# Attention on one core: the output stores go from SyncE's queue to GpSimd's, a pair of heads at a time

## The chip, the core and the metric

The kernel runs on one core of a Trainium2 chip. The core has TensorE (matrix products), VectorE, ScalarE (activations) and GpSimd for computing, and SyncE, which here only issues DMAs. SyncE, ScalarE and GpSimd can each issue DMAs; 16 DMA engines carry them out. Every engine works through its own instructions in order, and waits on semaphores for the others. The metric is the device time of one execution in microseconds (us); less is better. Before the change it is 1190.38 us, the median of three runs (1185.31, 1190.38 and 1191.48).

## The reference

```
B, H, Sq, Sk, D = 16, 32, 192, 1024, 128          # q, k, v in bfloat16
scores = einsum("bhqd,bhkd->bhqk", q, k) * D**-0.5
p      = softmax(scores, axis=-1)
return   einsum("bhqk,bhkd->bhqd", p, v)
```

There are 16 x 32 = 512 heads. Each has 192 queries, 1024 keys and 1024 values of 128 numbers. The inputs are 25.2 MB of q, 134.2 MB of k and 134.2 MB of v; the output is 25.2 MB.

## The kernel before

**Tiling.** 512 heads are 32 groups (`NGR`) of 16 heads (`G`), and a group is 8 pairs of heads (`PPG`). A pair has 2 x 192 = 384 queries, which are three units of 128: A (the first 128 of head a), B (the last 128 of head b) and S (64 left over from each). Two pairs make six units, A0 B0 A1 B1 S0 S1, and one *period* of the order that is written out by hand in `PE_ORDER`, `DVE_ORDER` and `ACT_ORDER` (lines 17 to 20). A tick behind a name there means that the step belongs to the period before, two ticks the one before that. So a group is four periods and 24 units (`UPG`).

**A unit's way.** TensorE makes its scores into `s_ps` (`qk`). VectorE copies them to `ss`, scaled and negated, and takes the row maximum (`rowmax`, L333). For units A0 and B1 GpSimd subtracts the maximum (`shift`, L208) and ScalarE takes the exponential later; for the other four ScalarE does both at once (`exp_first`, L374). TensorE transposes the result into `pt_ps` (`tr`), ScalarE brings it to `pt_sb` (`evac`, L383 and L385), and TensorE multiplies it with the values into `o_ps` (`pv`). When the three units of a pair are done, VectorE divides by the row sums and writes the pair's output to `ob` (`outputs`, L358), which adds one to the semaphore `s_on`.

**Buffers.** The transposed keys `kt` and queries `qt`, the values `vs` and the outputs `ob` have two buffers each, for two groups.

**DMA queues.** SyncE issues the loads of K (L148) and Q (L152), both as DMA transposes, and the stores (L172). Its program is: the first loads; then for each group g, `loads(g + 2)`, which waits until TensorE has made the last scores of group g (`s_qk`), and `stores(g, 0, 8)`, which waits until all outputs of group g are in `ob`. So behind the loads of a group stand the stores of the group two before it, and the next loads stand behind these. A group's output is 128 partitions of 8 x 3 rows of 256 bytes. It is stored as three DMAs, over partitions 0 to 79, 80 to 123 and 124 to 127 (`STORE_PARTS`). The last group is stored in four steps over all partitions as its pairs come out.

ScalarE issues the loads of V from group 2 on (L138, called at L394): in the middle of group g - 1, behind the evacuation of its thirteenth unit, it waits for the last PV product of group g - 2 (L392) and for K of group g to have landed (L393), and then issues V of group g. While it waits there, nothing else runs on ScalarE.

VectorE waits, before the first output of a group (L354), for the stores of the group that had the same half of `ob`. GpSimd does nothing but two shifts a period.

Of the kernel before, what the change touches and what calls it, by code (L numbers as in the profile page):

```python
# [22 lines left out]
def _order(text, periods):  # L23
    ops = [(w.split(":")[0], w.split(":")[1].rstrip("'"), w.count("'")) for w in text.split()]
    for p in range(periods + max(back for _, _, back in ops)):
        for op, name, back in ops:
            if 0 <= p - back < periods:
                if name in UNITS:
                    yield op, 6 * (p - back) + UNITS.index(name)
                else:  # L30
                    yield op, 2 * (p - back) + int(name)


def _attention_kernel(nc, q, k, v, out, G=16, NS=2, NSS=5, NX=4, NPT=5,
                      FIRST=((0, 2), (2, 8), (8, 16)), LAST=((0, 4), (4, 6), (6, 7), (7, 8)), STORE_PARTS=((0, 80), (80, 124), (124, 128)), VALUES_AFTER=("ev", 12)):
    B, H, SQ, D = q.shape
    SK = k.shape[2]
    assert D == 128 and SK == 1024 and SQ == 192, (D, SK, SQ)
# [2 lines left out]
    NGR = NH // G  # L41
    PPG = G // 2
# [5 lines left out]
    NSO = 2  # L48
# [5 lines left out]
    of = out.rearrange("b h s d -> (b h) s d")  # L54

    def shifted(u):
        return UNITS[u % 6] in SHIFTED
# [12 lines left out]
    with ExitStack() as es:  # L70
        def sb(name, shape, dt):
            return es.enter_context(nc.sbuf_tensor(name, shape, dt))
# [4 lines left out]
        def sem(name):  # L77
            return es.enter_context(nc.semaphore(name))
# [4 lines left out]
        ob = sb("ob", [128, NSO, PPG, 3, 128], BF16)  # L83
# [14 lines left out]
        svl = [sem("svl%d" % i) for i in range(NS)]  # L98
        sf = [sem("sf%d" % i) for i in range(len(FIRST))]
        sfv = [sem("sfv%d" % i) for i in range(len(FIRST))]  # L100
        sst = [sem("sst%d" % i) for i in range(NSO)]
        s_qk = sem("s_qk")
        s_max = sem("s_max")
        s_xa = sem("s_xa")
# [5 lines left out]
        s_on = sem("s_on")  # L110
# [3 lines left out]
        def unit_info(u):  # L114
            name = UNITS[u % 6]
            pr = 2 * (u // 6) + int(name[1])
            return pr, "ABS".index(name[0]), pr // PPG, pr % PPG
# [7 lines left out]
            return 16 * (g // NS + 1 - (g % NS == 0))  # L125

        def store_cnt(g):
            return 16 * len(STORE_PARTS) * (g // NSO + 1)

        def wait_x(eng, u):  # L130
            eng.wait_ge(s_xp if shifted(u) else s_xa, x_cnt[u])

        def pair_units(pr):
            return [u for u in range(6 * (pr // 2), 6 * (pr // 2) + 6) if unit_info(u)[0] == pr]

        def load_v(e, g, a, b, sm):
            h0 = g * G
            e.dma_start(  # L138
                vs[:, g % NS, a:b],
                vf[h0 + a:h0 + b].rearrange("g (p t) d -> p g t d", t=KT_TILES),  # L140
            ).then_inc(sm, 16)

        @block.sync
        def _(e):
            def load_kq(g, a, b, sems):
                s = g % NS
                h0 = g * G
                e.dma_start_transpose(  # L148
                    kt[:, s, :, a * 128:b * 128],
                    kf[h0 + a:h0 + b].rearrange("g (p t) d -> (g p) (t d)", t=KT_TILES),  # L150
                ).then_inc(sems[0], 16)
                e.dma_start_transpose(  # L152
                    qt[:, s, a * SQ:b * SQ],
                    qf[h0 + a:h0 + b].rearrange("g r d -> (g r) d"),
                ).then_inc(sems[1], 16)

            def loads(g):
                s = g % NS
                last_u = (g - NS + 1) * UPG - 1
                if g >= NS:  # L160
                    e.wait_ge(s_qk, last_u + 1)
                load_kq(g, 0, G, (sxk[s], sxq[s]))
                if g < NS:
                    load_v(e, g, 0, G, svl[s])

            def stores(g, a, b):
                so = g % NSO
                e.wait_ge(s_on, g * PPG + b)
                rows = of[g * G + 2 * a:g * G + 2 * b].rearrange("h r d -> (h r) d").rearrange(
                    "(n p) d -> p n d", p=128)  # L170
                for lo, hi in (((0, 128),) if g == NGR - 1 else STORE_PARTS):
                    e.dma_start(  # L172
                        rows[lo:hi],
                        ob[lo:hi, so, a:b].rearrange("p pg y d -> p (pg y) d"),
                    ).then_inc(sst[so], 16)

            n = len(FIRST)
            for i in range(n):
                load_kq(0, *FIRST[i], (sf[i], sf[i]))
                if i > 0:  # L180
                    for i2 in range(i if i > 1 else 0, i + 1):
                        load_v(e, 0, *FIRST[i2], sfv[i2])
            for g in range(1, min(NS, NGR)):
                loads(g)
            for g in range(NGR):
                if g + NS < NGR:
                    loads(g + NS)
                for a, b in (LAST if g == NGR - 1 else ((0, PPG),)):
                    stores(g, a, b)
            for so in range(min(NSO, NGR)):  # L190
                n = len(range(so, NGR - 1, NSO)) * len(STORE_PARTS)
                if so == (NGR - 1) % NSO:
                    n += len(LAST)
                e.wait_ge(sst[so], 16 * n)

        @block.gpsimd
        def _(gp):
            gp.memset(ones[:], 1.0).then_inc(s_setup, 1)  # L198
            gp.wait_ge(s_setup, 1)
            gp.affine_select(  # L200
                ident[:], ones[:], [[1, 128]], ALU.is_equal, 0.0, base=0, channel_multiplier=-1
            ).then_inc(s_setup, 1)

            def shift(u):
                gp.wait_ge(s_max, u + 1)
                if u >= NX:
                    gp.wait_ge(s_tr, u - NX + 1)
                gp.tensor_tensor(  # L208
                    x_sb[:, u % NX, :], ss[:, u % NSS, :],
                    nb[:, u % NSS: u % NSS + 1].to_broadcast([128, SK]), ALU.subtract,  # L210
                ).then_inc(s_xp, 1)

            for u in range(NU):
                if shifted(u):
                    shift(u)

        @block.tensor
        def _(pe):
# [19 lines left out]
            def qk(u):  # L238
# [13 lines left out]
                if g == 0:  # L252
                    for i, (h, _) in enumerate(FIRST):
                        if h <= b and i not in seen_kq:
# [72 lines left out]
        @block.vector  # L327
        def _(dve):
            def rowmax(u):
                dve.wait_ge(s_qk, u + 1)  # L330
                if u >= NSS and UNITS[u % 6] == "S1":
                    wait_x(dve, u - NSS)
                dve.tensor_scalar(  # L333
                    ss[:, u % NSS, :], s_ps[u % 2][:].rearrange("p t k -> p (t k)"), -scale, None, ALU.mult, ALU.min,
                    accum_out=nb[:, u % NSS: u % NSS + 1],
                ).then_inc(s_max, 1)

            def slots_of(pr, way):
                slots = sorted(O_SLOT[unit_info(u)[1]] for u in pair_units(pr) if shifted(u) == way)
                return slice(slots[0], slots[-1] + 1)  # L340

            def sums(pr):

                dve.wait_ge(s_xa, max(x_cnt[u] for u in pair_units(pr) if not shifted(u)))
                sel = slots_of(pr, False)
                dve.reciprocal(rinv[:, pr % 2, sel], rs[:, pr % NRS, sel]).then_inc(s_ri, 1)  # L346

            def outputs(pr):
                g = pr // PPG
                pg = pr % PPG  # L350
                so = g % NSO
                dve.wait_ge(s_pv, max(pv_cnt[u] for u in pair_units(pr)))
                if pg == 0 and g >= NSO:
                    dve.wait_ge(sst[so], store_cnt(g - NSO))  # L354
                sel = slots_of(pr, True)
                dve.reciprocal(rinv[:, pr % 2, sel], o_ps[pr % 2][:, 3, sel]).then_inc(s_ri, 1)  # L356
                dve.wait_ge(s_ri, 2 * pr + 2)
                dve.tensor_tensor(  # L358
                    ob[:, so, pg],
                    o_ps[pr % 2][:, 0:3, :],  # L360
                    rinv[:, pr % 2, 0:3].unsqueeze(2).to_broadcast([128, 3, 128]),
                    ALU.mult,
                ).then_inc(s_on, 1)

            do = {"max": rowmax, "sum": sums, "out": outputs}
            for op, u in _order(DVE_ORDER, NU // 6):
                do[op](u)
# [65 lines left out]
```

## Time and profile before

| | |
|---|---|
| median of three runs | 1190.38 us |
| the profiled execution, time | 1188.88 us |
| the profiled execution, span | 1187.1 us |
| granted clock of TensorE | 0.993 |
| TensorE products / VectorE / ScalarE / GpSimd busy | 1125.9 / 1087.6 / 1080.6 / 485.8 us |
| DMA traffic | 321.26 MB, mean 271 GB/s |
| queue q1 (SyncE): K, Q, stores, first V loads | 728257 packets, 192.95 MB |
| queue q10 (ScalarE): V loads | 61920 packets, 125.83 MB |

The page also lists who waited for whom. TensorE's busy time is modelled from pipelined products, so its 95% does not say that it is at its peak. A DMA issue shown on SyncE's queue lasts until SyncE can go on to its next instruction, not until the data has landed. The DMA share in a stretch of time adds up packets and can pass 1. The stores' landing times are not told by the page.

### The profile page before, as it was taken

The numbers are of one execution on the slowest core, as the hardware profiler recorded it, in microseconds if no ns is written. First come the engines' busy times: TensorE is split into PE (matmuls) and PEld (weight loads), VectorE is DVE, ScalarE is ACT, GpSimd is POOL, SyncE is SP. The second block draws the span as 40 slices with busy tenths as digits, with TensorE's granted clock in tenths as the row PEclk, the third lists the DMA queues.
The fourth block names the chain that finished last, engine by engine and source line by source line (L and its number), as shares of the span: only waits on it lengthen the run. The fifth ranks groups of instructions, "written<-read, shape, count | busy, mean of one in ns | idle before, by whom it ended". The sixth has DMA issues, their size and how long they took to land.

```text
span 1187.1 us, 38884 instructions
## 1 busy us (share of the span) xinstructions
PE 1125.9 (95%) x18432; PEld 845.9 (71%) x15360; DVE 1087.6 (92%) x2304; ACT 1080.6 (91%) x1793; POOL 485.8 (41%) x262
## 2 busy tenths in 40 slices
PE   5699999999999999999999999999999999999998
PEld 2477776777777776777777767777777776677776
DVE  5589998999999998999999989999999999899997
ACT  4679998999999998999999988999999998899998
POOL 2234443444444434443444434344444343444442
PEclk9899999999999999999999999999999999999999
DMA  9999999999999999999999999999999999999981
GB/s 231 249 280 303 289 285 254 260 299 293 287 293 248 256 290 288 280 283 258 279 298 284 284 265 242 290 296 282 288 266 267 295 284 290 259 267 277 297 246 40
DMA packets 790348, 321.26 MB, mean 271 GB/s; under 512 B 724641, under 2 KB 724641, under 8 KB 790177
## 3 DMA queue, kind: packets, MB, share of 16 engines
q1 hardware_dynamic: 728257, 192.95, 84.0%
q10 hardware_dynamic: 61920, 125.83, 28.7%
q8 instruction: 132, 2.16, 0.7%
q14 instruction: 39, 0.32, 0.1%
HBM read 134.22 MB, written 25.17 MB: 134 GB/s over the span
## 4 chain that ended last, share of the span: by engine, by line
PE 43%; DMA 39%; ACT 11%; SPq 5%; ACTq 1%; issue 0%; DVE 0%
DMA kt<-in_k_dram 39%; PE o_ps L221 15%; PE pt_ps L221 15%; PE s_ps L221 14%; ACT x_sb L374 6%; SPq L148 4%; ACT pt_sb L385 3%; ACT pt_sb L383 2%; ACTq L138 1%; SPq L152 1%; SPq L138 0%; DMA vs<-in_v_dram 0%; DVE ob L358 0%; ACTq L393 0%; DVE rinv L356 0%
## 5 line engine op out<-in xcount | busy, mean ns | idle before, releaser
L333 DVE TENSOR_SCALAR_CACHE_REDUCE ss<-s_ps 128x1024 f32<-128x1024 f32 x768 | 919.5, 1220 | 83.2 <-PE s_ps L221 69.7
L208 POOL TENSOR_TENSOR x_sb<-ss,nb 128x1024 bf16<-128x1024 f32 x256 | 485.1, 1895 | 689.3 <-DVE ss L333 574.1
L374 ACT ACTIVATE x_sb<-ss,nb 128x1024 bf16<-128x1024 f32 x512 | 584.9, 1144 | 13.0 <-DVE ss L333 13.0
L306 PEld LDWEIGHTS <-pt_sb 128*128 128x128 bf16 (+1 forms) x8192 | 440.9, 104 | 194.9 <-issue 101.7
L221 PE MATMUL o_ps<-vs,pt_sb 128*128 128x128 bf16 (+1 forms) x8192 | 494.9, 219 | 0.4 <-DMA vs<-in_v_dram 0.3
L221 PE MATMUL s_ps<-kt,qt 128*128 128x512 bf16 (+1 forms) x2048 | 465.2, 385 | 24.2 <-DMA qt<-in_q_dram 23.7
L221 PE MATMUL pt_ps<-ident,x_sb 128*128 128x128 bf16 x6144 | 449.9, 220 | 33.4 <-ACT pt_sb L383 15.9
L280 PEld LDWEIGHTS <-x_sb 128*128 128x128 bf16 x6144 | 368.9, 98 | 101.5 <-issue 100.7
L385 ACT ACTIVATE pt_sb<-pt_ps 128x512 f32<-128x512 f32 x512 | 306.3, 598 | 84.6 <-PE pt_ps L221 51.5
L383 ACT ACTIVATE pt_sb<-pt_ps 128x1024 bf16<-128x1024 bf16 x256 | 260.3, 1017 | 3.6 <-PE pt_ps L221 3.6
L221 PE MATMUL o_ps<-ones,pt_sb 128*128 128x1 bf16 x2048 | 189.3, 165 | 0.0
L358 DVE TENSOR_TENSOR ob<-o_ps,rinv 128x384 bf16<-128x384 f32 x256 | 142.6, 557 | 8.7
L264 PEld LDWEIGHTS <-qt 128*128 128x128 bf16 (+1 forms) x1024 | 79.3, 103 | 41.6 <-DMA qt<-in_q_dram 18.7
L374 ACT ACTIVATION_READ_ACCUMULATOR x_sb<-ss,nb 128x1 f32 x512 | 100.3, 196 | 0.0
L333 DVE DVE_READ_ACCUMULATOR ss<-s_ps 128x1 f32 x768 | 63.7, 83 | 0.0
L356 DVE RECIPROCAL rinv<-o_ps 128x1 f32<-128x1 f32 x256 | 41.8, 163 | 4.3 <-PE o_ps L221 4.3
L346 DVE RECIPROCAL rinv<-rs 128x2 f32<-128x2 f32 x256 | 41.0, 160 | 1.1 <-ACT x_sb L374 1.1
L374 ACT ACT_TABLE_LOAD x1 | 1.3, 1283 | 0.8 <-PEq L418 0.8
L200 POOL TENSOR_SCALAR_AFFINE_SELECT ident<-ones 128x128 bf16<-128x128 bf16 x1 | 0.3, 294 | 0.1
L198 POOL MEMSET ones<- 128x128 bf16 x1 | 0.2, 205 | 0.3 <-POOLq L418 0.3
L418 POOL MEMSET const-float32-0.0<- 128x1 f32 x1 | 0.1, 99 | 0.3 <-issue 0.3
L418 POOL MEMSET const-bfloat16-1.0<- 128x1 bf16 x1 | 0.1, 102 | 0.0
(2 smaller groups left out, 0.2 us busy)
## 6 DMA issues: line engine op xcount, KB each, us to landing
vs<-in_v_dram ACTq DMA_DIRECT2D x30, 4096.0 KB, 16.3
out_dram<-ob SPq DMA_DIRECT2D x31, 480.0 KB
out_dram<-ob SPq DMA_DIRECT2D x31, 264.0 KB
vs<-in_v_dram SPq DMA_DIRECT2D x1, 4096.0 KB, 15.1
vs<-in_v_dram SPq DMA_DIRECT2D x1, 2048.0 KB, 10.4
vs<-in_v_dram SPq DMA_DIRECT2D x1, 1536.0 KB, 8.9
out_dram<-ob SPq DMA_DIRECT2D x31, 24.0 KB
kt<-in_k_dram SPq DMA_TRANSPOSE x34, 21.1
```

What stands on the lines that cost most here:

```text
L148: e.dma_start_transpose(kt[:, s, :, a * 128:b * 128], kf[h0 + a:h0 + b].rearrange("g (p t) d -> (g p) (t d)", t=KT_TILES),).then_inc(sems[ ...
L208: gp.tensor_tensor(x_sb[:, u % NX, :], ss[:, u % NSS, :], nb[:, u % NSS: u % NSS + 1].to_broadcast([128, SK]), ALU.subtract,).then_inc(s_x ...
L221: return pe.add_instruction(mybir.InstMatmult(name=nc.get_next_instruction_name(), engine=mybir.EngineType.PE, ins=[pe.lower_ap(x), pe.low ...
L264: pe.ldweights(w, tile_position=at)
L280: pe.ldweights(w, is_transpose=True, tile_position=(0, 0))
L306: pe.ldweights(w, tile_position=at)
L333: dve.tensor_scalar(ss[:, u % NSS, :], s_ps[u % 2][:].rearrange("p t k -> p (t k)"), -scale, None, ALU.mult, ALU.min, accum_out=nb[:, u % ...
L356: dve.reciprocal(rinv[:, pr % 2, sel], o_ps[pr % 2][:, 3, sel]).then_inc(s_ri, 1)
L358: dve.tensor_tensor(ob[:, so, pg], o_ps[pr % 2][:, 0:3, :], rinv[:, pr % 2, 0:3].unsqueeze(2).to_broadcast([128, 3, 128]), ALU.mult,).then ...
L374: act.activation(x_sb[:, u % NX, :], ss[:, u % NSS, :], ACT_FN.Exp, bias=nb[:, u % NSS: u % NSS + 1], scale=-1.0, accum_out=rs[:, pr % NRS ...
L383: act.activation(pt_sb[:, u % NPT], pt_ps[u % 2][:], ACT_FN.Exp, scale=-1.0).then_inc(s_ev, 1)
L385: act.activation(words(pt_sb[:, u % NPT]), words(pt_ps[u % 2][:]), ACT_FN.Copy).then_inc(s_ev, 1)
```

## The change

For all groups but the last, GpSimd issues the stores. After each of its shifts it issues one DMA, which stores partitions 0 to 120 of one pair of heads: 121 partitions of 3 rows of 256 bytes. The pair is one whose period lies three back (`STORE_LAG`), and GpSimd waits for its output first. That makes 248 DMAs on GpSimd's queue, two in each period. SyncE stores the other seven partitions, 121 to 127, of the whole group in one DMA, where its three stores stood before. The semaphore `ssp` counts GpSimd's stores; VectorE waits for it beside `sst` before it writes over a half of `ob`, and SyncE at the end. The order of the instructions on TensorE, VectorE and ScalarE stays as it was.

```diff
-    ... STORE_PARTS=((0, 80), (80, 124), (124, 128)), VALUES_AFTER=("ev", 12)):
+    ... BY_PAIRS=121, STORE_LAG=3, VALUES_AFTER=("ev", 12)):
...
+        ssp = [sem("ssp%d" % i) for i in range(NSO)]
...
         def store_cnt(g):
-            return 16 * len(STORE_PARTS) * (g // NSO + 1)
+            return 16 * (g // NSO + 1)
...
+        def store(e, g, a, b, lo, hi, sm):
+            rows = of[g * G + 2 * a:g * G + 2 * b].rearrange("h r d -> (h r) d").rearrange("(n p) d -> p n d", p=128)
+            e.dma_start(
+                rows[lo:hi],
+                ob[lo:hi, g % NSO, a:b].rearrange("p pg y d -> p (pg y) d"),
+            ).then_inc(sm[g % NSO], 16)
...
             def stores(g, a, b):
-                so = g % NSO
                 e.wait_ge(s_on, g * PPG + b)
-                rows = of[g * G + 2 * a:g * G + 2 * b].rearrange("h r d -> (h r) d").rearrange(
-                    "(n p) d -> p n d", p=128)
-                for lo, hi in (((0, 128),) if g == NGR - 1 else STORE_PARTS):
-                    e.dma_start(
-                        rows[lo:hi],
-                        ob[lo:hi, so, a:b].rearrange("p pg y d -> p (pg y) d"),
-                    ).then_inc(sst[so], 16)
+                store(e, g, a, b, 0 if g == NGR - 1 else BY_PAIRS, 128, sst)
...
                 e.wait_ge(sst[so], 16 * n)
+                e.wait_ge(ssp[so], 16 * PPG * len(range(so, NGR - 1, NSO)))
...
+            stored = (NGR - 1) * PPG
             for u in range(NU):
                 if shifted(u):
                     shift(u)
+                    pr = 2 * (u // 6 - STORE_LAG) + (u % 6 > 0)
+                    if 0 <= pr < stored:
+                        gp.wait_ge(s_on, pr + 1)
+                        store(gp, pr // PPG, pr % PPG, pr % PPG + 1, 0, BY_PAIRS, ssp)
...
                 if pg == 0 and g >= NSO:
                     dve.wait_ge(sst[so], store_cnt(g - NSO))
+                    dve.wait_ge(ssp[so], PPG * store_cnt(g - NSO))
```

More of the change, by code (lines that the diff above doesn't have):

```diff
@@ L34, in _attention_kernel @@
 def _attention_kernel(nc, q, k, v, out, G=16, NS=2, NSS=5, NX=4, NPT=5,
-                      FIRST=((0, 2), (2, 8), (8, 16)), LAST=((0, 4), (4, 6), (6, 7), (7, 8)), STORE_PARTS=((0, 80), (80, 124), (124, 128)), VALUES_AFTER=("ev", 12)):
+                      FIRST=((0, 2), (2, 8), (8, 16)), LAST=((0, 4), (4, 6), (6, 7), (7, 8)), BY_PAIRS=121, STORE_LAG=3, VALUES_AFTER=("ev", 12)):
     B, H, SQ, D = q.shape
@@ L190, in _ @@
             for so in range(min(NSO, NGR)):
-                n = len(range(so, NGR - 1, NSO)) * len(STORE_PARTS)
+                n = len(range(so, NGR - 1, NSO))
                 if so == (NGR - 1) % NSO:
```

## The prediction

> **What bounds the kernel now.** I read the page first: every compute engine is over 90% busy, and the DMA row is at nine tenths in nearly every slice, so shares alone do not say who leads.
>
> ```profile
> PE 1125.9 (95%) x18432; PEld 845.9 (71%) x15360; DVE 1087.6 (92%) x2304; ACT 1080.6 (91%) x1793; POOL 485.8 (41%) x262
> ...
> DMA  9999999999999999999999999999999999999981
> ...
> L333 DVE TENSOR_SCALAR_CACHE_REDUCE ss<-s_ps 128x1024 f32<-128x1024 f32 x768 | 919.5, 1220 | 83.2 <-PE s_ps L221 69.7
> L208 POOL TENSOR_TENSOR x_sb<-ss,nb 128x1024 bf16<-128x1024 f32 x256 | 485.1, 1895 | 689.3 <-DVE ss L333 574.1
> ```
>
> Then GpSimd in order of time, because it works once every half period and so shows the pace. Columns: start, duration, what, and in brackets the idle time before it.
>
> ```profile
> 175.32 1.89 POOL L208 TENSOR_TENSOR x_sb<-ss,nb 128x1024 bf16<-128x1024 f32 x1 [2.44 <-DVE ss L333]
> 179.62 1.89 POOL L208 TENSOR_TENSOR x_sb<-ss,nb 128x1024 bf16<-128x1024 f32 x1 [2.40 <-DVE ss L333]
> 183.96 1.90 POOL L208 TENSOR_TENSOR x_sb<-ss,nb 128x1024 bf16<-128x1024 f32 x1 [2.45 <-DVE ss L333]
> ```
>
> The reader is to see two things: a period of six units takes 183.96 - 175.32 = 8.64 us when nothing disturbs it, and GpSimd idles 2.4 us after each shift. Four periods make a group: 34.56 us. But the chain of work that ended last has the K loads of groups 4 and 29 starting at 140.29 and 1041.94 us:
>
> ```profile
> 140.29 20.43 DMA kt<-in_k_dram
> ...
> 1041.94 21.07 DMA kt<-in_k_dram
> ```
>
> That is 901.65 us for 25 groups, 36.07 us each, so 1.5 us of every group is lost. Where, the SyncE queue and ScalarE in order of time show, for one group (its predecessor's last scores, the x4 row, end at 168.01 us; I call this T):
>
> ```profile
> 167.41 0.60 PE L221 MATMUL s_ps<-kt,qt 128*64 128x512 bf16 x4
> ...
> 163.22 12.59 SPq L172 DMA_DIRECT2D out_dram<-ob  x2
> 175.86 19.15 SPq L148 DMA_TRANSPOSE kt<-in_k_dram  x1
> 195.05 3.97 SPq L152 DMA_TRANSPOSE qt<-in_q_dram  x1
> 199.06 13.71 SPq L172 DMA_DIRECT2D out_dram<-ob  x3
> 212.81 18.32 SPq L148 DMA_TRANSPOSE kt<-in_k_dram  x1
> ...
> 194.84 1.01 ACT L383 ACTIVATE pt_sb<-pt_ps 128x1024 bf16<-128x1024 bf16 x1
> 198.68 0.38 ACTq L138 DMA_DIRECT2D vs<-in_v_dram  x1
> 199.10 0.60 ACT L385 ACTIVATE pt_sb<-pt_ps 128x512 f32<-128x512 f32 x1 [3.25 <-DMA kt<-in_k_dram]
> ```
>
> SyncE's queue is never empty: K 19.15, Q 3.97, stores 13.71, at once the next K. The slot for K is free at T, but K is issued at T + 7.85, when the stores before it are through the queue. ScalarE reaches its wait for that K (L393, ahead of the V load) at 195.85 = T + 27.84, and K only lands at about 198.6: 3.25 us of idle ScalarE, which then holds back TensorE and VectorE. So the bound is the chain stores, K, V, stores through SyncE's queue, and compute pays where it waits for K.
>
> **The change, part by part.** The sum is made against the profiled execution's 1188.88 us (span 1187.1), 0.13% under the median 1190.38 of the three runs.
>
> *Stores leave SyncE's queue.* Three issues of 13.7 us a group go. Two of them are long because they stand in a full queue behind Q and beside V. K can then be issued at T instead of T + 7.85 (T + 7.5 is typical: 6.1 us after the next group's first scores, which are 1.4 us behind T). What is late next is worked out from the transfer rates of four stretches:
>
> ```profile
> 184.00:188.00 4.00, 4.00 (x80) 3.01 (x63) 3.97 (x7) 4.00 (x8) 1.86 (x1) 1.00 1.28 290
> 196.00:198.00 2.00, 1.56 (x26) 1.15 (x16) 1.92 (x4) 0.00 (x0) 1.10 (x1) 1.00 1.56 150
> 206.00:212.00 6.00, 6.00 (x96) 4.72 (x74) 5.89 (x13) 6.00 (x11) 1.94 (x2) 1.00 1.08 389
> 214.00:216.00 2.00, 2.00 (x31) 1.20 (x20) 1.97 (x5) 2.00 (x5) 1.10 (x1) 1.00 0.52 122
> ```
>
> The last column is GB/s: K runs at 290, V with stores at 389, and there are holes (150 inside K, 122 between the end of the stores and K's start). A group's K and Q are 4.19 + 0.79 MB, 17.2 us at 290; V and stores the same bytes, 12.8 us at 389: 30.0 us of transfer in a period of 34.56. So the engines have the room; it is the order, with its holes, that makes 36.
>
> *When K lands now.* V would be issued when ScalarE gets there, T + 27.8, run from about 2.8 us later (issue 198.68, 389 GB/s after 201.5) and need (4.19 + 0.25 MB of stores) / 389 = 11.4 us: it ends at T + 42, which is 7.4 us into the next group. K, issued at 0 of that group, gets little until then; today it waits for the stores' tail till about 3.2 us after its issue (216 - 212.81). Median from issue to landing is 21.1 us, so K lands at 21.1 + (7.4 - 3.2) = 25.3, and 0.4 MB of stores mixed into it at 290 add 1.4: 26.7, against 27.8 when ScalarE asks. Just in time; landings scatter by some 1.5 us, so a tenth of a microsecond a group, 3 us in all, stays lost. V lands at about 8.4 us of the next group, first used near its 11th (PV of unit A0 is in the second period): covered by 2 us. Q lands 5 us after K and is needed at 34.6.
>
> *What that is worth.* First scores of group 2 are at 98.8 us and of group 31 at 1142.1: 1043.3 us for 29 groups, less 29 x 34.56 = 41 us lost. The first of these waits (1.2 us) is for a K with no store ahead of it and stays. Gain 40 - 3 = 37 us.
>
> *Stores on GpSimd.* 248 DMAs of 363 rows of 256 B, one behind each shift. The trace of before has no DMA issue on GpSimd, so the price x is bounded. It can't be a gain, the engine has to do something. Low end: 0.38 us, the issue of a V load by ScalarE. High end: 6.6 us, one of the two long store issues of SyncE, (13.71 - 0.6)/2. Between them I go by GpSimd's own pace, to which it is nearest: 1.89 us for 1024 elements of a row is 1.85 ns a step; 363 rows at two steps each, one for the read and one for the write, are 1.3 us, and with the engine's memset (0.2 us) for its start 1.5 us, an estimate. Up to 2.43 us it lies wholly in the idle time shown above and costs nothing; beyond that GpSimd becomes the bound, and a period is 2 x (1.89 + x). It breaks even where 124 periods lose 41 us, 0.33 each: x = 2.6. So this one number decides the sign. A store delays the next shift only if it outlasts the gap; transposes of A0 come some 6 us after its shift.
>
> GpSimd and VectorE may also get in each other's way. VectorE is busy 92% of the span, in pieces of 1.22 us (L333); a store that has to sit out one such piece takes 1.5 + 1.22 = 2.7 us and is past the limit. Against it: the shifts of GpSimd run beside the same pieces and take 1.89 us each time. The Trainium skill's page "SBUF — State Buffer", section "SBUF: two separate sides", has such a rule: GpSimd can't write descriptors while VectorE holds the port that they share in a two-port mode, and a store of about 620 ns took about 3100 ns beside one. By 3.1 us the sum would be 1314, by 0.62 us it would be the one below. The page exempts `tensor_scalar` when it also writes its accumulator, which L333 does, so I leave the rule out of the sum.
>
> *Waits that are added.* GpSimd waits for s_on of a pair three periods back, made by VectorE at least half a period (4.3 us) earlier: nothing. VectorE's new wait on ssp is for stores issued over two periods (17 us) before: behind it would stand the row maxima, but a store lands far sooner than that even at the 16.3 us of a V load. *Partitions 121 to 127 on SyncE:* 42 KB, one issue between 0.6 and 6.6 us; SyncE is idle from about T + 22 + that until 34.6: hidden. *Order on the other engines* is unchanged. *The end:* the last group's stores are as before.
>
> Sum: 1188.9 - 37 + 0 = 1152 us.
>
> **Rivals.** (a) *GpSimd becomes the bound* (slower). For it: 363 descriptors made one by one are much work for 2.4 us of room, and the program has to do it twice a period. Against: idle 59% of the span. With four steps a row instead of two x is 363 x 4 x 1.85 ns + 0.2 = 2.9 us, a period is 9.58: 1188.9 - 41 + 124 x 0.94 = 1264 us. With a store that sits out one piece of VectorE's (x = 2.7), 1188.9 - 41 + 124 x 0.54 = 1215 us. The skill's rule on the shared port, named above, is this second form.
> (b) *The transfers only change places.* Stores mixed into K cost it more than their bytes, since K's stream already shows holes; at 3 us instead of 1.4 K lands at 28.3, 0.5 late and 0.7 with the scatter: 29 x 0.7 = 20 us of the 40 come back, 1169 us.
> (c) *Nothing changes.* Stores take the same 16 DMA engines, and the row with 9s is full; if the 36 us are engine time and not queue order, the time stays at 1188. Against it: 122 and 150 GB/s in the holes. The skill's page "DMA: Bandwidth & Descriptors", section "Issuing engines are not separate DMA queues", says just this: another issuer saves the sequencer's time alone, usually small. Here the trace has that time at 13.7 us a group in the queue that K needs.
>
> **How the numbers follow.** Forecast 0.52 (1152, by itself 1144 to 1161: no loss left and the runs' spread, or 0.4 us a group left); (b) 0.12, faster too; (c) 0.08; (a) 0.28, of which 0.06 the form with VectorE. A measurement here tells 0.5%, 6 us, from nothing. Faster 0.64, same 0.08, slower 0.28. The range runs from 1142 (the whole loss gone, from the fastest run's side) to 1240 (x = 2.8), which leaves out about two in ten, nearly all above.
>
> **What would show it.** Right: K issues start within 1 us of the last scores of the group before; the wait of ScalarE for kt is gone; shifts come every 4.32 us in all four periods of a group; DMA issues on GpSimd take under 2.4 us. Wrong: shifts on GpSimd that start right at the end of a DMA issue, with VectorE or TensorE waiting for x_sb from GpSimd; or K landing as late as before with a flatter GB/s row, which would be (b) or (c).

## The result, and the profile after

The changed kernel takes 1291.14 us (median of four runs, 1284.74 to 1298.37) against 1190.91 for the kernel before: the ratio is 1.0855, with a 95% interval from 1.0789 to 1.0921. It is slower, and neither the forecast nor the range (1142 to 1240) held it. The profiled execution took 1290.87 us, 102 us more than the one before.

The page of the changed kernel, with the lines that answer to those shown before; in part 6 the last number is the median time from issue to landing:

```profile
PE 1158.9 (90%) x18432; PEld 870.5 (68%) x15360; DVE 1089.1 (84%) x2304; ACT 1081.3 (84%) x1793; POOL 694.3 (54%) x510
...
q0 software_dynamic: 15872, 23.23, 7.2%
...
DMA kt<-in_k_dram 71%; PE o_ps L228 6%; PE s_ps L228 6%; PE pt_ps L228 6%; SPq L156 4%; ACT x_sb L382 2%; ACT pt_sb L393 2%; ACT pt_sb L391 1%; ACTq L139 1%; SPq L160 1%; SPq L139 0%; DMA vs<-in_v_dram 0%; DVE ob L366 0%; ACTq L401 0%; DVE rinv L364 0%
...
L146 POOL DMA_DIRECT2D out_dram<-ob x248 | 222.1, 895 | 0.0
...
vs<-in_v_dram ACTq DMA_DIRECT2D x30, 4096.0 KB, 16.3
out_dram<-ob POOLq DMA_DIRECT2D x248, 90.8 KB, 7.5
...
kt<-in_k_dram SPq DMA_TRANSPOSE x34, 31.2
```

A store costs GpSimd 0.895 us, far inside its 2.4 us gap, and GpSimd is busy 54%: it is not the bound. What changed is K. Its load takes 31.2 us from issue to landing, where the median was 21.1, and the K loads now hold 71% of the chain (39% before).

GpSimd, SyncE and ScalarE in order of time, the changed kernel (columns as before: start, duration, what, idle time before it):

```profile
305.29 1.88 POOL L210 TENSOR_TENSOR x_sb<-ss,nb 128x1024 bf16<-128x1024 f32 x1 [1.60 <-DVE ss L340]
307.13 0.90 POOL L146 DMA_DIRECT2D out_dram<-ob  x1
309.59 1.88 POOL L210 TENSOR_TENSOR x_sb<-ss,nb 128x1024 bf16<-128x1024 f32 x1 [1.56 <-DVE ss L340]
311.43 0.89 POOL L146 DMA_DIRECT2D out_dram<-ob  x1
313.92 1.88 POOL L210 TENSOR_TENSOR x_sb<-ss,nb 128x1024 bf16<-128x1024 f32 x1 [1.60 <-DVE ss L340]
...
181.94 27.46 SPq L156 DMA_TRANSPOSE kt<-in_k_dram  x1
209.45 4.75 SPq L160 DMA_TRANSPOSE qt<-in_q_dram  x1
214.24 0.48 SPq L146 DMA_DIRECT2D out_dram<-ob  x1
221.69 26.78 SPq L156 DMA_TRANSPOSE kt<-in_k_dram  x1
...
208.74 1.01 ACT L391 ACTIVATE pt_sb<-pt_ps 128x1024 bf16<-128x1024 bf16 x1
213.86 0.37 ACTq L139 DMA_DIRECT2D vs<-in_v_dram  x1
214.28 0.60 ACT L393 ACTIVATE pt_sb<-pt_ps 128x512 f32<-128x512 f32 x1 [4.54 <-DMA kt<-in_k_dram]
```

The undisturbed period is still 8.63 us (313.92 - 305.29), so GpSimd does not lengthen it. The granted clock drops to half for some 3 us behind the wait shown here (214.9 to 218.3 us); 19 of its 21 drops lie within 2.5 us of a landing of K, and its mean is 0.959 against 0.993. It does not set the pace: a group is as long as its V and K loads (see the table below). SyncE's queue is now idle for 6 to 8 us ahead of each K (here 214.72 to 221.69), and K is issued the moment the group before has its last scores. But the K issued at 181.94 lands at about 213.8, 31.8 us later, and ScalarE, which was done with the step before its wait at 209.75, stands still for 4.54 us. In the lists of waits, before and after, ScalarE's for K (in total, times, longest):

```profile
ACT pt_sb L385 <- DMA kt<-in_k_dram: 25.9, 12, 3.3
...
ACT pt_sb L393 <- DMA kt<-in_k_dram: 122.1, 29, 6.3
```

The rates tell why. Two stretches of the changed kernel inside K transfers, without and with a store under way (last column GB/s, K and store together):

```profile
201.00:202.00 1.00, 1.00 (x16) 0.74 (x12) 1.00 (x1) 1.00 (x3) 0.00 (x0) 1.00 1.27 292
308.00:311.00 3.00, 3.00 (x54) 2.36 (x35) 2.89 (x9) 3.00 (x6) 1.44 (x2) 1.00 1.27 168
```

K alone runs at 290. While one store of 0.093 MB trickles through, all of it falls to 168, with some 140 of it K's.

### The profile page after: what moved, and what is told of

The parts are those of the page before. It is cut to its first block, busy times and chain, and to the rows that moved or that the text cites. A ratio compares the mean times of both kernels' runs of the same rounds, so it can differ in the third digit from the quotient of the medians.

```text
span 1289.1 us, 39071 instructions
## 1 busy us (share of the span) xinstructions
PE 1158.9 (90%) x18432; PEld 870.5 (68%) x15360; DVE 1089.1 (84%) x2304; ACT 1081.3 (84%) x1793; POOL 694.3 (54%) x510
## 4 chain that ended last, share of the span: by engine, by line
DMA 71%; PE 17%; ACT 5%; SPq 4%; ACTq 1%; issue 0%; DVE 0%
DMA kt<-in_k_dram 71%; PE o_ps L228 6%; PE s_ps L228 6%; PE pt_ps L228 6%; SPq L156 4%; ACT x_sb L382 2%; ACT pt_sb L393 2%; ACT pt_sb L391 1%; ACTq L139 1%; SPq L160 1%; SPq L139 0%; DMA vs<-in_v_dram 0%; DVE ob L366 0%; ACTq L401 0%; DVE rinv L364 0%
## 5 line engine op out<-in xcount | busy, mean ns | idle before, releaser
L340 DVE TENSOR_SCALAR_CACHE_REDUCE ss<-s_ps 128x1024 f32<-128x1024 f32 x768 | 920.1, 1220 | 183.5 <-PE s_ps L228 169.3
L313 PEld LDWEIGHTS <-pt_sb 128*128 128x128 bf16 (+1 forms) x8192 | 451.0, 105 | 205.9 <-issue 111.9
L228 PE MATMUL pt_ps<-ident,x_sb 128*128 128x128 bf16 x6144 | 465.1, 224 | 100.1 <-ACT pt_sb L393 91.2
L228 PE MATMUL o_ps<-vs,pt_sb 128*128 128x128 bf16 (+1 forms) x8192 | 506.1, 221 | 1.2 <-DMA vs<-in_v_dram 1.1
L228 PE MATMUL s_ps<-kt,qt 128*128 128x512 bf16 (+1 forms) x2048 | 478.2, 392 | 25.7 <-DMA qt<-in_q_dram 25.2
L287 PEld LDWEIGHTS <-x_sb 128*128 128x128 bf16 x6144 | 381.9, 100 | 166.1 <-issue 165.6
L146 POOL DMA_DIRECT2D out_dram<-ob x248 | 222.1, 895 | 0.0
L340 DVE DVE_READ_ACCUMULATOR ss<-s_ps 128x1 f32 x768 | 63.6, 83 | 0.0
## 6 DMA issues: line engine op xcount, KB each, us to landing
kt<-in_k_dram SPq DMA_TRANSPOSE x34, 31.2
```

The source lines that it names most:

```text
L146: e.dma_start(rows[lo:hi], ob[lo:hi, g % NSO, a:b].rearrange("p pg y d -> p (pg y) d"),).then_inc(sm[g % NSO], 16)
L228: return pe.add_instruction(mybir.InstMatmult(name=nc.get_next_instruction_name(), engine=mybir.EngineType.PE, ins=[pe.lower_ap(x), pe.low ...
L287: pe.ldweights(w, is_transpose=True, tile_position=(0, 0))
L313: pe.ldweights(w, tile_position=at)
L340: dve.tensor_scalar(ss[:, u % NSS, :], s_ps[u % 2][:].rearrange("p t k -> p (t k)"), -scale, None, ALU.mult, ALU.min, accum_out=nb[:, u % ...
```

## The experiments

Theory M: a store that meets K holds it up by far more than its bytes, about 1 us. Rival O: K issued early runs into the V load, and those two spoil each other. Later rivals: the form of GpSimd's stores; their shape; bytes against rows. The table has, for all runs, the mean over groups 3 to 31 of two times from the landings in the trace: V from issue to landing, and K from the landing of the V before it to its own. Where the text says "by the packets", it counts the DMA packets, for each of which the trace has queue, start, time and size; a store meets K when its data moves between V's landing and K's. Wherever ScalarE waits for K, V is issued as K lands, so the two add up to a group; about 34.5 us is the least that compute allows (run 1, where nothing waits for K, has 34.54 between the first scores of one group and the next). The edits are against the changed kernel and cut to the lines that matter; "..." stands for the rest.

| kernel | V, issue to landing | then K | sum, us | time, us |
|---|---|---|---|---|
| before | 16.35 | 19.56 | 35.9 | 1190.9 |
| changed | 16.51 | 22.69 | 39.2 | 1291.1 |
| 1 no GpSimd stores | 15.38 | 17.86 | 33.2 | 1147.0 |
| 2 K after V | 15.53 | 23.78 | 39.3 | 1294.9 |
| 3 stores beside V, too late | 17.17 | 22.84 | 40.0 | 1312.0 |
| 4 128 partitions | 16.45 | 20.97 | 37.4 | 1237.8 |
| 5 stores from ScalarE | 15.88 | 21.39 | 37.3 | 1233.8 |
| 6 stores beside V, earlier | 19.18 | 17.31 | 36.5 | 1211.5 |
| 7 the same, 128 partitions | 18.40 | 17.74 | 36.1 | 1198.2 |
| 8 17 partitions | 16.32 | 24.33 | 40.7 | 1336.2 |
| 9 64 partitions | 16.60 | 19.12 | 35.7 | 1187.0 |
| 10 four and four | 18.60 | 17.54 | 36.1 | 1199.7 |
| 11 80 from SyncE, 48 from GpSimd | 17.09 | 18.82 | 35.9 | 1187.8 |
| 12 112 and 16 | 16.70 | 19.56 | 36.3 | 1199.8 |

Runs 1 to 9 are one execution each; runs 1, 8 and 9 stand against the changed kernel, not against the one before, since they write less. The kernel before, taken again beside these runs, was at 1182.1 us (one execution) beside runs 1 to 7, 1189.3 (median of seven) beside 8 to 10 and 1188.2 (median of 13) beside 11 and 12.

**1. No GpSimd stores.**

```diff
-                    if 0 <= pr < stored:
-                        gp.wait_ge(s_on, pr + 1)
-                        store(gp, pr // PPG, ...)
...
```

> GpSimd's stores are left out (the output of partitions 0 to 120 is not written, but for the last group); all else as in the changed kernel. Theory M (each GpSimd store that meets the K transfer holds it up by about 1 us, some 6 stores a K): K lands about 25 us after its issue instead of 31, ScalarE's wait for K is gone, the period is 8.64 us throughout, about 1150 us. Rival O (K issued right at the last scores runs into the V load of the group before, and the two spoil each other beyond their bytes): K still takes about 30 us, above 1250 us.

1147.0 us, and K lands 25.3 us after its issue. Theory M holds, and O falls: K still runs into V (V lands 7.5 us after K's issue), and no time is lost by it.

**2. K after V.**

```diff
                     e.wait_ge(s_qk, last_u + 1)
+                    e.wait_ge(svl[(g - 1) % NS], load_cnt(g - 1))
```

> The changed kernel, with SyncE also waiting for V of the group before to have landed before it issues K. M: K still meets the stores, 24 to 25 us from issue to landing, and now starts later: a group is V 15.5 + K 25 = 40.5 us, about 1330 us. O: K takes 20 us as before the change, a group 36 us, about 1190 us.

K takes 23.7 us from issue to landing though V is out of the way, so O falls again; the time, 1294.9, is below M's 1330: V took the 15.5 us that M gave it, but K 23.7 instead of 25, and 39.3 us a group is some 1295 us.

**3. Stores beside V.**

```diff
-    NSO = 2
+    NSO = 3
...
-                    pr = 2 * (u // 6 - STORE_LAG) + (u % 6 > 0)
...
+                    if p % 4 in (3, 0) and p >= 7:
+                        first = PPG * ((p - 7) // 4) + 4 * (p % 4 == 0) + 2 * (u % 6 > 0)
+                        for pr in (first, first + 1): ...
```

> GpSimd issues the same 248 stores, but two behind each shift of the last period of a group and the first of the next, where V is being loaded, and none behind the others (a third output buffer, so that nothing waits for them). Two issues of 0.9 us fit the gap of 2.4 us. M: K is met by few stores and lands about 26 us after its issue, in time or nearly so; 1150 to 1175 us. O: no change against the changed kernel, about 1290 us. If a store costs as much beside V as beside K, V lands late, K with it, and the time stays near 1290 us too.

A miss: 1312.0 us, K no better. The placement was wrong by the store's own delay. In the packets of the changed kernel the first full packet of a store moves 5.1 us (median) after the start of GpSimd's issue, and for eight stores in ten 3.6 to 6.7 us after it. So the stores meant for the second half of V met K: by their packets, 4.3 of the eight of a group.

**4. All 128 partitions from GpSimd.**

```diff
-BY_PAIRS=121
+BY_PAIRS=128
...
-                for a, b in (LAST if g == NGR - 1 else ((0, PPG),)):
+                for a, b in (LAST if g == NGR - 1 else ()):
...
```

> GpSimd stores all 128 partitions of each pair and SyncE none. Rival S (the shape: 121 partitions reach only some of the DMA engines, and each of these is held longer): with the rows spread evenly a store costs K half as much, K lands 27 to 28 us after its issue, 1200 to 1230 us. M without S: within 15 us of the changed kernel's 1291.

1237.8 us, with more bytes from GpSimd than in the changed kernel: faster than M without S has it, but not in the range of S. In the packets, a store of 121 partitions is 22 of 4096 bytes and 11 of 256: 33 rows on each of 11 DMA engines. 128 partitions are 16 of 4096 and 16 of 2048: 24 rows on each of 16. K loses 3.1 us to them instead of 4.8, and by their packets 5.4 stores meet a K instead of 5.8: 0.58 us a store instead of 0.83. So the shape is about a third of the damage (53 us of the 144 between the changed kernel and run 1); SyncE's small store, gone here too, was not tried by itself. (The Trainium skill's page "DMA: Bandwidth & Descriptors", section "Why a DMA increments its semaphore by 16 and not by 1", says that a DMA uses the largest number of engines up to 16 that divides its outermost size; 121 gives 11, as seen. It also tells of some copies from GpSimd that are split unevenly over 16; that was not so here.)

**5. The same stores from ScalarE.**

```diff
...
+                if op == "ev" and shifted(u):
+                    pr = 2 * (u // 6 - STORE_LAG) + (u % 6 > 0)
+                    ... store(act, pr // PPG, pr % PPG, pr % PPG + 1, 0, BY_PAIRS, ssp)
```

> The same 248 stores of a pair over all 128 partitions, but issued by ScalarE (behind the evacuation of A0 and of B1) and none by GpSimd or SyncE. Each issue costs ScalarE some 0.4 us, so its period grows to about 9.5 us and the time is not to be compared; what counts is K from issue to landing: 25.3 us without stores, 29.9 with the same stores from GpSimd. If any store that meets K costs this much: 29 to 30 us. If it is the form of GpSimd's stores (packets of up to 4096 bytes where SyncE's are 256): 26 to 27 us, the bytes alone.

K takes 29.6 us. ScalarE's stores go in packets of 256 bytes, 384 a store, and cost K as much as GpSimd's in 32 packets of 2048 and 4096: 0.63 and 0.58 us for each store that meets it. It is not GpSimd's way of storing, nor the number of packets; it is storing while K moves.

**6 and 7. Beside V, earlier; with 121 and with 128 partitions.**

```diff
+                    gap = (u // 3) % 8
+                    first, n = {5: (0, 3), 6: (3, 3), 7: (6, 2)}.get(gap, (0, 0))
+                    g = u // UPG - 1
+                    for pg in range(first, first + n): ...
```

> The changed kernel (121 partitions) with the eight stores of a group moved to three gaps of GpSimd (3, 3 and 2 stores, behind the shift of B1 in the third period and of A0 and B1 in the fourth), earlier than in the run before by one gap and more, since a store moves its data only 4 to 5 us after its issue: now they should meet V and hardly K. If a store costs much only beside K: K lands 26 us or less after its issue, ScalarE's wait for K is gone or small, V takes 16.5 us; 1150 to 1175 us. If a store costs as much beside V: V takes 19 us and more, K starts to move later and lands as late as in the changed kernel; 1250 us or more.

> The same placement with all 128 partitions from GpSimd and none from SyncE. If shape and placement both count: a little faster than the 121-partition form, 1145 to 1165 us. If placement does nothing: 1238 us, as with 128 partitions spread over the period.

1211.5 and 1198.2 us, both outside what was expected. Placed so, the stores no longer touch K (by their packets, 0.03 and 0.14 of the eight of a group meet it): 17.3 and 17.7 us from V's landing, as without stores. A stretch of run 7 with V and stores, and one with K alone:

```profile
314.00:317.00 3.00, 3.00 (x64) 2.18 (x49) 2.97 (x7) 3.00 (x6) 2.83 (x3) 1.00 1.05 383
329.00:333.00 4.00, 4.00 (x75) 2.90 (x68) 3.93 (x10) 3.76 (x6) 1.88 (x1) 1.00 1.27 290
```

In such a stretch V and the stores run at 383 GB/s together. Over the whole V load a store costs more than its bytes, but less than beside K: V now takes 18.4 us in run 7 where it took 15.4, 0.38 us a store (98 KB at 383 GB/s would be 0.26), and 19.2 in run 6, 0.48 a store. K waits for V, V's successor is issued when K lands, and a group of run 7 is 36.1 us again: nearly what the kernel before had.

**8 and 9. Rows on the busiest engine against bytes.**

```diff
-store(gp, pr // PPG, pr % PPG, pr % PPG + 1, 0, BY_PAIRS, ssp)
+store(gp, pr // PPG, pr % PPG, pr % PPG + 1, 0, 17, ssp)     # run 8; 64 in run 9
```

> The changed kernel, but each store of GpSimd covers partitions 0 to 16 only, a seventh of its bytes (17 to 120 are not written, but for the last group). 121 partitions went as 33 rows on each of 11 DMA engines (22 packets of 4096 bytes a store); 17 should go as 51 rows on a single one (three packets of 4096 bytes). Theory L (K's transposes need all 16 engines in step, so a store costs K what its rows take on the busiest engine, 27 ns a row by the runs so far): 1.4 us a store, K lands later than in the changed kernel, above 1310 us. Rival B (a store costs by its bytes): 0.13 us a store, K as without stores, 1147 to 1155 us. If the packets show that the 17 partitions are spread over many engines, both expect little.

> As the run before it with partitions 0 to 63: half the bytes, 12 rows on each of 16 engines (64 to 120 are not written, but for the last group). L: 12 x 27 ns = 0.33 us a store, K 19.4 us from the end of V to its landing (17.9 without stores, 21.0 with 24 rows, 22.7 with 33), 1150 to 1165 us. If the number of stores counts and not their rows: as with 128 partitions, 1238 us.

Run 8 moves a seventh of the bytes and is the slowest of all, 1336.2 us. Its packets are three of 4096 bytes and one of 768 a store; they follow one another, so all 51 rows go through one engine (the trace does not name it). Part 3 and part 6 of its page, and two stretches of K: alone, and mostly between the packets of one store (322.65 to 323.20) and those of the next (from 324.84):

```profile
q0 software_dynamic: 19840, 4.01, 3.0%
...
out_dram<-ob POOLq DMA_DIRECT2D x248, 12.8 KB, 8.3
...
kt<-in_k_dram SPq DMA_TRANSPOSE x34, 32.5
```

```profile
321.00:322.00 1.00, 1.00 (x23) 0.66 (x20) 0.97 (x4) 0.76 (x3) 0.18 (x1) 1.00 1.27 290
323.00:325.00 2.00, 2.00 (x35) 1.60 (x25) 1.97 (x7) 2.00 (x5) 1.73 (x2) 1.00 1.29 151
```

A store of 13 KB takes one of the 16 engines for some 0.6 us, and the whole transfer falls from 290 to 151 GB/s. Were the other 15 engines free to go on, it would stay above 270. And it stays low when the store's data is through: over 31 stores of run 8 that move inside K, with no other store and no instruction fetch near, the median rate is 115 to 145 GB/s from 0.5 to 1.5 us after the store's first packet and above 260 again from 1.75 us. That the DMA transpose moves its 16 engines in step would explain it, but the trace does not tell the engines apart, so this is an inference. What is shown is the price, which follows the rows on the busiest engine and not the bytes. By the packets 5.0, 5.4, 5.8 and 6.2 stores meet a K in the runs with 12, 24, 33 and 51 rows; against 17.86 us without them, each costs 0.25, 0.58, 0.83 and 1.05 us: 21 to 25 ns a row. The rows are not all: run 3's stores, of 33 rows too but issued two at a time, cost K 1.2 us each, and why was not tried. Run 9's K agrees with its forecast (19.1 for 19.4 us), its time does not (1187 for 1150 to 1165): V also took 1.2 us more, and V is half of the loop.

**10, 11 and 12. Looking for a faster version.** Run 10 is run 7 with the stores as four and four in two gaps. Runs 11 and 12 leave 80 or 112 partitions with SyncE in one DMA per group and give GpSimd the rest, in the three gaps.

```diff
-{5: (0, 3), 6: (3, 3), 7: (6, 2)}                            # run 10
+{5: (0, 4), 6: (4, 4)}
-store(e, g, a, b, 0 if g == NGR - 1 else BY_PAIRS, 128, sst)  # runs 11 and 12
+store(e, g, a, b, 0, 128 if g == NGR - 1 else BY_SYNC, sst)
```

> All 128 partitions from GpSimd, eight stores of a group in two gaps (four and four, behind the shift of B1 in the third period and of A0 in the fourth) instead of three, so that the last ones have moved before the next K is issued. Four issues take 3.0 us, 0.6 more than the gap, which the slack of the shifts should bear. If what was left over the kernel before (1198 against 1182) is the mixture of V, stores and K at the end of V: V 17.4 us, K 17.5 us from V's end, a group 35.0 us, 1155 to 1170 us, faster than the kernel before. If V and stores together with K simply fill the DMA engines: a group 36 us, 1185 to 1200 us.

> A version that follows from the runs: SyncE stores partitions 0 to 79 of a group in its old place (one issue, which took 0.6 us before the change and does not hold up K), and GpSimd the other 48, 9 rows on each of 16 engines a pair, in the three gaps beside V. A group has been V's issue to landing plus V's landing to K's in every run in which ScalarE waits for K. Expected: V 17.5 (15.4, 1.0 for SyncE's rows as before the change, 1.1 for GpSimd's 72 rows at 15.6 ns, its price beside V), K 17.7 as in the runs with stores beside V: 35.2 us a group instead of 36.0 before the change, about 1168 us. If GpSimd's stores near the end of V still spoil K's start: 36 us a group or more, 1190 us.

> The same with 112 partitions from SyncE and 16 from GpSimd (3 rows on each engine a pair). SyncE's issue may be held by its full queue for some us but ends before the next K is due. Expected: V 16.6, K 18.5 (40 of SyncE's rows a DMA engine outlast V and stand ahead of K, 14 ns each): 35.1 us a group, about 1165 us. If SyncE's issue is held beyond the last scores of the group, K starts late as before the change: 36 us a group, 1190 us.

1199.7 us (ratio to the kernel before 1.0101, 1.0056 to 1.0146), 1187.8 (0.9997, 0.9975 to 1.0019) and 1199.8 (1.0081, 1.0059 to 1.0104). None beats the kernel before. In run 10 V took 18.6 us instead of 17.4. In run 11 SyncE's store issues take 0.6 us and K goes out at the last scores, as expected; V took 17.1, but K 18.8 instead of 17.7, and in run 12 K took 19.6 instead of 18.5; why was not looked into. Five ways of placing 0.79 MB of stores beside V (the kernel before, 7, 10, 11, 12) all end between 35.9 and 36.3 us a group.

## Why the prediction was wrong

*The bound* was read rightly: ScalarE's wait for K behind SyncE's queue. Run 1 shows that without it, and without stores, the time is 1147, close to the 1188.9 - 41 us that the prediction put on the loss.

*Stores leave SyncE's queue, K is issued at T*: right to the tenth of a microsecond.

*When K lands now* failed, and it decided the result. Its term for the stores mixed into K was 1.4 us, by bytes at 290 GB/s. It measured 4.8 us (22.69 - 17.86), and V, met by other stores, took 1.1 us more. Leaving out the 1.4, the step has K landing 25.3 us after its issue, and run 1 measured 25.3. That K moves once V has landed was right: 21.1 - 3.2 = 17.9 us for it, measured 17.86. That V's landing came out too (7.4 us after K's issue, measured 7.5) is partly luck, as two misses cancel: ScalarE, when nothing holds it, issues V 26.6 us after the last scores in run 1 and not 27.8, and V takes 15.4 us and not 14.2. The earlier issue also means that the forecast's margin of 1.1 us (27.8 - 26.7) was not there. A DMA transpose beside stores was priced by bytes like any other transfer, and the place where the trace of before had stores, beside V at 389 GB/s, does not show what they cost beside K.

*The engines have the room* (30.0 us of transfer in 34.56) failed too. Rates from the best stretches left out the holes as if order made them. But both holes that the prediction shows, at 196 to 198 and 214 to 216 us, begin in the packets just behind a fetch of instructions (at 196.50 and 214.80 us), and run 1 has such holes too, with K issued at once and no stores from GpSimd. In run 1 V and K take 33.2 us a group, so only 1.3 us is free, and the whole output's stores take at least 2.7 in every placement tried. None of these gives 1152.

*Stores on GpSimd* were taken at 1.5 us and called the number that decides the sign. They measured 0.895, and 0.51 to 1.07 in the other shapes; the sign was decided elsewhere. VectorE did not hold them up either: 894 ns is both the least and the median of 248. The Trainium skill's page "SBUF — State Buffer", section "Who interferes with whom", exempts the form of `tensor_scalar` that also writes its accumulator, which is L333's, now L340; the trace agrees with that, at 894 ns with VectorE busy 84% of the span.

*The added waits, SyncE's small store and the end* cost nothing, as worked out: in the list of waits of the changed kernel none is on a store but SyncE's last, 1.4 us.

*The rivals.* (a) named the right direction with the wrong cause: no shift waits for a store's issue. (b) had the mechanism, K's stream spoilt by the stores, with 3 us where 4.8 came, and so a gain instead of a loss: with 3 us the prediction's own sum has K 0.5 us late. With the measured 4.8 us, plus 1.1 more for V, K lands at 25.3 + 5.9 = 31.2 us, 3.4 behind the 27.8 of the prediction and 4.6 behind the 26.6 of run 1; a group grew from 34.5 to 39.2 us, by 4.7. (c) was wrong for this change (39.2 us a group), but it is nearly what the best placement gives: the same engines, the same 36 us. The rule of the Trainium skill that the prediction names beside it (page "DMA: Bandwidth & Descriptors", section "Issuing engines are not separate DMA queues"), that another issuing engine only saves the sequencer's time, fits runs 4 and 5, where the stores of GpSimd and of ScalarE left K at nearly the same 20.97 and 21.39 us; the section says nothing of a transpose in the way.

## What to carry to other kernels

Before a small transfer is moved to another queue, look at what it will run beside and not only at what it stood behind: behind K in one queue the stores were held away from it, on a queue of their own they met it. Beside a DMA transpose, price a small transfer by its rows on the busiest engine and not by its bytes (21 to 25 ns a row in these runs), and choose a partition count that spreads over all 16. Take a stream's real time from a run or stretch with its holes in it; the best rate shown is not the room that is there.

## What the runs showed of the hardware

A DMA transpose loses far more time than the bytes of a DMA that meets it would take: a store of 13 KB, through one engine in some 0.6 us, took a K stream of 290 GB/s to 115 to 145 for a microsecond (run 8). A row of 256 bytes cost K 21 to 25 ns there, about twice what its packet takes by itself (178 ns for 16 rows in the changed kernel). Why the stream takes so long to recover was not tried.

A store from GpSimd of at most 128 rows of 768 bytes holds the engine 0.5 to 1.1 us, and its time follows the rows on an engine more than the bytes: 0.513 us for 16 partitions (3 rows on an engine), 0.655 for 64 (12), 0.785 for 128 (24), 0.894 for 121 (33), 1.071 for 17 (51). Its data moves only some 5 us after the start of the issue, with the queues as full as they are here.

K's stream also has holes without any store, as this stretch of run 1 between two clean ones shows:

```profile
312.00:314.00 2.00, 2.00 (x40) 1.36 (x32) 1.97 (x5) 2.00 (x5) 1.49 (x1) 1.00 1.28 290
315.00:316.00 1.00, 1.00 (x16) 0.65 (x11) 0.93 (x4) 1.00 (x2) 0.11 (x1) 1.00 0.13 6
317.00:322.00 5.00, 5.00 (x87) 3.71 (x80) 4.90 (x13) 4.76 (x8) 2.56 (x2) 1.00 1.27 290
```

In the packets of run 1, a 16 KB fetch of instructions (queue q8, 132 in the whole span) starts about half a microsecond before nearly every such hole, at 314.46 us here; there are about two to a K load, each of about a microsecond. That fits a transpose in step, waiting for the one engine that fetches, but no run here took the fetches away.
